# Linear attention and a Sinkhorn-routed mixture of experts: fp16, transposes by DMA, and attention pipelined with the first expert

## The chip, the cores and the metric

The kernel runs on one core of one Trainium2 chip. The metric is device time in microseconds (us), as the median of several executions; lower is better. All executions that are compared here were of the same, undisturbed state ("fast"). The profile is one execution, taken by the hardware profiler.

Names of engines in the profile: PE is the matmul engine and PEld its weight load, DVE the vector engine, ACT the scalar engine, POOL the GpSimd engine, SP the sync engine. "SPq" or "POOLq" is the same engine issuing a DMA.

## The reference

Eight batches, 8 heads, 576 positions, head width 64; then 4608 tokens of width 512 through 8 experts of hidden width 1024, all in fp32.

```python
def phi(x, c, s):                       # c, s: cos and sin of the position
    r = np.maximum(x, 0.0)
    return np.concatenate([r * c, r * s], axis=-1)        # 64 -> 128 features
q_p, k_p = phi(q, cos_w, sin_w), phi(k, cos_w, sin_w)
kv  = np.einsum('bhsf,bhsd->bhfd', k_p, v)
z   = np.sum(k_p, axis=2)
num = np.einsum('bhsf,bhfd->bhsd', q_p, kv)
den = np.einsum('bhsf,bhf->bhs', q_p, z)[..., None] + 1e-06
x   = (num / den) rearranged to (4608 tokens, 512)

P = np.exp(x @ w_gate - max)            # 4608 x 8
for _ in range(8):                      # Sinkhorn
    P /= P.sum(1, keepdims=True) + 1e-09
    P /= P.sum(0, keepdims=True) + 1e-09
    P *= N / E
for e in range(8):
    out += P[:, e:e + 1] * (np.maximum(x @ w1[e], 0.0) @ w2[e])
```

## The kernel before

It runs in three stages, one after the other: attention for all batches, which leaves x transposed in SBUF (`xT`); gates and Sinkhorn; the experts. The parts that matter here:

```python
for b in range(B):
    for hk in range(NPAIR):                            # two heads at a time
        # loads of q, k, v in fp32 on SP's queue, 2304 bytes a row (q: 256)
        nc.scalar.copy(out=q_ld[:, :, 1, :], in_=q_ld[:, :, 0, :])
        nc.vector.tensor_copy(out=v_aug[:, :, 0:D], in_=v_ld[:])      # v and a column of ones
        # k_p = max(k, 0) * (cos | sin), two DVE operations
        for hh in range(2):
            for c in range(CH):                                       # CH = 9
                nc.tensor.matmul(out=kv_ps[:, hh, :], lhsT=k_p[...], rhs=v_aug[...], ...)
        # q transposed on PE, fp32, 9 times; DVE applies max and cos | sin
        nc.tensor.transpose(out=tr_ps[:, i, :], in_=q_ld[:, c], identity=ident_f[:])
        nc.vector.scalar_tensor_tensor(out=q_pT[:, hh, s0:s0+ln], in0=tr_ps[...], ...)
        # numerator and denominator in one matmul; 1/den per token; scaled by ACT into st
        nc.tensor.matmul(out=num_ps[:rows, si, :], lhsT=q_pT[...], rhs=kv_sb[:, hh, :], ...)
        nc.vector.reciprocal(out=rden[...], in_=num_ps[:rows, si, D:D+1])
        nc.scalar.activation(out=st[...], in_=num_ps[...], func=AF.Copy, scale=rden[...])
        nc.tensor.transpose(out=x_ps[...], in_=st[...], identity=ident_bf[...])   # x^T on PE
        # copied to xT
# ... gates, 8 Sinkhorn rounds ...
for e in range(E):                                     # experts outer
    for j in range(NJ):                                # 9 chunks of 512 tokens
        # h_ps (4 buffers) = w1e^T x^T: 32 matmuls of 128x512; ACT: Relu into hT (bf16)
        # y_ps (2 buffers) = hT^T w2e: 32 matmuls of 128x512; DVE: out_acc += P * y_ps
```

The softmax here doesn't subtract the row's maximum and nothing guards it: scores larger than these inputs give would overflow.

## Time and profile before

| | before |
|---|---|
| time, median of 3 executions | 1244.44 us (1241.79 to 1244.47) |
| first expert matmul (`h_ps`) | about 228 us |
| 4608 expert matmuls of 128x512 at 0.2155 us, start to start | 993 us |
| last `y_ps` ends | 1235.4 us of the profiled 1241.5 |

The page of the kernel before. The rows of digits are the span in 40 equal slices, each digit the busy share in tenths; PEclk is the clock granted to PE in tenths. After the chain come groups of instructions: count, then total busy time and mean ns of one, then the idle time before them and who ended it.

```profile
span 1241.5 us, 15196 instructions
PE 1189.6 (96%) x6128; PEld 580.1 (47%) x6128; DVE 431.4 (35%) x1158; ACT 466.3 (38%) x1051; POOL 1.8 (0%) x10
...
PE   5898888899999999999999999999999999999998
...
PEclk9999999999999999999999999999999999999999
DMA  9847440400030003000300030003000100001122
...
PE 89%; DVE 7%; issue 2%; ACT 1%; DMA 0%; SPq 0%; DVEq 0%; ACTq 0%
...
L397 PE MATMUL h_ps<-xT,w1e 128*128 128x512 bf16 x2304 | 515.0, 380 | 0.0
...
L262 PE MATMUL tr_ps<-ident_f,q_ld 128*128 128x128 f32 x288 | 89.1, 440 | 6.3 <-ACT q_ld L213 5.7
...
L247 PE MATMUL kv_ps<-v_aug,k_p 64*128 64x65 bf16 x576 | 43.1, 239 | 31.8 <-DVE k_p L232 24.4
...
L312 PE MATMUL x_ps<-ident_bf,st 128*128 128x128 bf16 (+1 forms) x160 | 33.9, 278 | 4.5 <-ACT st L302 3.0
```

PE is busy 96% of the time, at full clock throughout, and PE is 89% of the chain of work that ended last. But the lines of `tr_ps` and `x_ps` are work that computes nothing: 448 transposes, 123 us of PE busy time. Attention is the first eight slices.

Busy time by stretch of the kernel before: each line is a stretch, its length, then busy us of each engine with the count of instructions, the granted clock, the DMA share and GB/s.

```profile
0.00:100.00 100.00, 75.66 (x552) 51.96 (x552) 70.66 (x332) 53.71 (x187) 1.75 (x10) 1.00 0.77 222
...
400.00:600.00 200.00, 200.00 (x928) 90.69 (x927) 48.92 (x63) 67.18 (x113) 0.00 (x0) 1.00 0.06 22
```

In the attention no engine is full: PE 76, DVE 71 and ACT 54 of 100 us hand work to each other. Among the experts PE is full, and 928 matmuls take 200 us. That stretch is the floor; the 228 us in front of it are what can be won.

### The profile page before, as it was taken

Reading aid. Unit: us, or ns where it says so; the run is one execution under the profiler, and the core shown is the slowest. Engines: PE = TensorE matmul, PEld = TensorE weight load, DVE = VectorE, ACT = ScalarE, POOL = GpSimd, SP = SyncE. Lnnn points to the kernel's source line nnn. Section 1 sums busy time; section 2 is a strip of 40 time slices with the busy share of each in tenths; the row PEclk is TensorE's granted clock in tenths of the full one; section 3 lists DMA queues with packets and bytes.
Section 4 is the critical chain, followed back from the end, with each engine's and each line's share of the span. In section 5 each row is a group of like instructions: output and inputs, shape, how many; then the busy total and the mean of one; then the engine's idle time right before and its main releaser. Section 6 shows DMA issues by size and latency. Waiting matters only on the chain.

```text
span 1241.5 us, 15196 instructions
## 1 busy us (share of the span) xinstructions
PE 1189.6 (96%) x6128; PEld 580.1 (47%) x6128; DVE 431.4 (35%) x1158; ACT 466.3 (38%) x1051; POOL 1.8 (0%) x10
## 2 busy tenths in 40 slices
PE   5898888899999999999999999999999999999998
PEld 3555555444444444444444444444444444444443
DVE  6777777563232223222322232223222322212221
ACT  4554554541333333333333333333333333333332
POOL 0000000000000000000000000000000000000000
PEclk9999999999999999999999999999999999999999
DMA  9847440400030003000300030003000100001122
GB/s 301 218 134 211 127 132 2 137 1 1 1 115 22 1 1 113 23 1 1 112 25 1 1 110 27 1 1 108 29 1 1 68 1 1 1 1 68 68 80 90
DMA packets 64742, 72.30 MB, mean 58 GB/s; under 512 B 39584, under 2 KB 39584, under 8 KB 64672
## 3 DMA queue, kind: packets, MB, share of 16 engines
q1 hardware_dynamic: 64672, 71.33, 18.0%
q8 instruction: 48, 0.79, 0.3%
q14 instruction: 22, 0.18, 0.0%
HBM read 61.88 MB, written 9.44 MB: 57 GB/s over the span
## 4 chain that ended last, share of the span: by engine, by line
PE 89%; DVE 7%; issue 2%; ACT 1%; DMA 0%; SPq 0%; DVEq 0%; ACTq 0%
PE y_ps L413 40%; PE h_ps L397 39%; PE tr_ps L262 4%; PE kv_ps L247 3%; PE num_ps L285 2%; DVE k_p L232 2%; DVE v_aug L227 2%; DVE rden L296 1%; DVE q_pT L270 1%; DVE colp L359 0%; ACT kv_sb L254 0%; DMA v_ld<-in_v_dram 0%; PE x_ps L312 0%; DVE P_tok L352 0%; DVE rs L349 0%
## 5 line engine op out<-in xcount | busy, mean ns | idle before, releaser
L404 ACT ACTIVATE hT<-h_ps 128x512 bf16<-128x512 f32 x576 | 343.9, 597 | 649.7 <-PE h_ps L397 649.0
L397 PE MATMUL h_ps<-xT,w1e 128*128 128x512 bf16 x2304 | 515.0, 380 | 0.0
L413 PE MATMUL y_ps<-w2e,hT 128*128 128x512 bf16 x2304 | 509.2, 379 | 0.0
L430 DVE SCALAR_TENSOR_TENSOR out_acc<-y_ps,P_tok,out_acc 128x512 f32<-128x512 f32 x252 | 189.2, 751 | 620.8 <-PE y_ps L413 620.8
L413 PEld LDWEIGHTS <-hT 128*128 128x128 bf16 x2304 | 225.0, 98 | 271.4
L397 PEld LDWEIGHTS <-w1e 128*128 128x128 bf16 x2304 | 223.9, 98 | 266.1 <-issue 0.3
L262 PE MATMUL tr_ps<-ident_f,q_ld 128*128 128x128 f32 x288 | 89.1, 440 | 6.3 <-ACT q_ld L213 5.7
L302 ACT ACTIVATE st<-num_ps,rden 128x64 bf16<-128x64 f32 (+1 forms) x320 | 70.5, 313 | 42.0 <-DVE rden L296 39.2
L247 PE MATMUL kv_ps<-v_aug,k_p 64*128 64x65 bf16 x576 | 43.1, 239 | 31.8 <-DVE k_p L232 24.4
L270 DVE SCALAR_TENSOR_TENSOR q_pT<-tr_ps,cs2b 128x128 bf16<-128x128 f32 (+1 forms) x320 | 62.9, 260 | 0.2 <-PE tr_ps L262 0.2
L262 PEld LDWEIGHTS tr_ps<-ident_f,q_ld 128*128 128x128 f32 x288 | 48.4, 214 | 11.9 <-issue 5.7
L247 PEld LDWEIGHTS <-k_p 64*128 64x128 bf16 x576 | 32.3, 124 | 42.8 <-DVE k_p L232 28.6
L285 PE MATMUL num_ps<-kv_sb,q_pT 128*128 128x65 bf16 (+1 forms) x320 | 48.2, 251 | 0.2 <-DVE q_pT L270 0.2
L422 DVE TENSOR_SCALAR out_acc<-y_ps,P_tok 128x512 f32<-128x512 f32 x36 | 26.9, 750 | 60.0 <-PE y_ps L413 59.9
L296 DVE RECIPROCAL rden<-num_ps 128x1 f32<-128x1 f32 (+1 forms) x320 | 27.0, 151 | 54.0 <-PE num_ps L285 52.3
L232 DVE SCALAR_TENSOR_TENSOR k_p<-k_ld,cs 128x576 bf16<-128x576 f32 x64 | 45.2, 742 | 0.8 <-ACT cs L147 0.8
L285 PEld LDWEIGHTS <-q_pT 128*128 128x128 bf16 (+1 forms) x320 | 33.1, 134 | 19.0 <-issue 7.0
L312 PE MATMUL x_ps<-ident_bf,st 128*128 128x128 bf16 (+1 forms) x160 | 33.9, 278 | 4.5 <-ACT st L302 3.0
L254 ACT CAST kv_sb<-kv_ps 128x65 bf16<-128x65 f32 x64 | 13.8, 215 | 52.1 <-PE kv_ps L247 49.9
L108 DVE CAST w1e<-wst 128x2048 bf16<-128x2048 f32 x16 | 19.0, 1221 | 36.9 <-PE h_ps L397 36.9
L312 PEld LDWEIGHTS <-st 128*128 128x128 bf16 (+1 forms) x160 | 16.6, 106 | 29.0 <-ACT st L302 16.2
L227 DVE CAST v_aug<-v_ld 128x576 bf16<-128x576 f32 x32 | 23.2, 726 | 4.6 <-DMA v_ld<-in_v_dram 4.6
(62 smaller groups left out, 116.2 us busy)
## 6 DMA issues: line engine op xcount, KB each, us to landing
wst<-in_moe_w_dram SPq DMA_DIRECT2D x32, 1024.0 KB, 5.7
q_ld<-in_q_dram SPq DMA_DIRECT2D x32, 288.0 KB, 3.4
k_ld<-in_k_dram SPq DMA_DIRECT2D x32, 288.0 KB, 3.8
v_ld<-in_v_dram SPq DMA_DIRECT2D x32, 288.0 KB, 3.8
out_dram<-out_acc SPq DMA_DIRECT2D x9, 1024.0 KB, 4.3
wg_ld<-in_moe_w_gate_dram SPq DMA_DIRECT2D x1, 16.0 KB, 1.9
```

Of the source, the lines that this page charges most:

```text
L227: nc.vector.tensor_copy(out=v_aug[:, :, 0:D], in_=v_ld[:])
L232: nc.vector.scalar_tensor_tensor(out=k_p[:, :, a, :], in0=k_ld[:], scalar=0.0, in1=cs[:, :, a, :], op0=ALU.max, op1=ALU.mult,)
L247: nc.tensor.matmul(out=kv_ps[:, hh, :], lhsT=k_p[p0 : p0 + HP, c, :, :].rearrange("p a d -> p (a d)"), rhs=v_aug[p0 : p0 + HP, c, :], star ...
L262: nc.tensor.transpose(out=tr_ps[:, i, :], in_=q_ld[:, c, :, :].rearrange("p a d -> p (a d)"), identity=ident_f[:],)
L270: nc.vector.scalar_tensor_tensor(out=q_pT[:, hh, s0 : s0 + ln], in0=tr_ps[:, i, p0 : p0 + ln], scalar=0.0, in1=cs2b[:, s0 : s0 + ln], op0= ...
L285: nc.tensor.matmul(out=num_ps[:rows, si, :], lhsT=q_pT[:, hh, s0 : s0 + rows], rhs=kv_sb[:, hh, :], start=True, stop=True,)
L302: nc.scalar.activation(out=st[:rows, si, hh * D : (hh + 1) * D], in_=num_ps[:rows, si, 0:D], func=AF.Copy, scale=rden[:rows, si : si + 1],)
L312: nc.tensor.transpose(out=x_ps[:, s0 : s0 + rows], in_=st[:rows, si, :], identity=ident_bf[:rows, :rows],)
L397: nc.tensor.matmul(out=h_ps[:, :ntok], lhsT=w1e[:, kt, ft * P : (ft + 1) * P], rhs=xT[:, kt, tj0 : tj0 + ntok], start=(kt == 0), stop=(kt ...
L404: nc.scalar.activation(out=hT[:, ft, :ntok], in_=h_ps[:, :ntok], func=AF.Relu)
L413: nc.tensor.matmul(out=y_ps[:srows, :], lhsT=hT[:, ft, ts0 : ts0 + srows], rhs=w2e[:, ft, :], start=(ft == 0), stop=(ft == FT - 1),)
L430: nc.vector.scalar_tensor_tensor(out=out_acc[:srows, cidx, :], in0=y_ps[:srows, :], scalar=P_tok[:srows, cidx, e : e + 1], in1=out_acc[:sr ...
```

## The change

Its intent is to take the transposes off PE, and to start expert 0 as soon as a batch of x exists, so that PE has expert matmuls to do while the rest of the attention runs. The diff is large (nearly the whole file); this is its core, shortened, with some lines put in words and cuts marked by "...".

```diff
-BF16 operands, weights loaded in fp32 by SP and cast by DVE
+F16 operands; q, k, v and weights loaded by POOL's queue, cast to fp16 in the DMA
-h_ps: 4 buffers
+h_ps: 2 buffers (the room goes to the attention, which now runs beside it)
 ...
+def prep(b, hk):                       # 4 buffers of k_p, 2 of q_p, 7 of q_pT, 5 of each load
+    nc.vector.tensor_copy(out=v_aug[:, :, 0:D], in_=v16[:])
+    for x16, pool, name in ((k16, kp_pool, "k_p"), (q16, qp_pool, "q_p")):
+        nc.scalar.activation(out=x16[:], in_=x16[:], func=AF.Relu)
+        nc.vector.tensor_tensor(out=x_p[:], in0=x16 (repeated), in1=cs[:], op=ALU.mult)
-        nc.tensor.transpose(out=tr_ps[:, i, :], in_=q_ld[:, c], identity=ident_f[:])
+    nc.sync.dma_start_transpose(out=q_pT[:], in_=q_p[:])           # 128 x 1152 fp16
+    if b + 1 < B:
+        load(b + 1, hk)
+def denominators(b, zsel):
+    # den_ps[head, token]: 24 small matmuls of 192 columns a batch
+    nc.vector.tensor_scalar(out=den[:], in0=den_ps[...], scalar1=1e-6 / XS, op0=ALU.add)
+    nc.vector.reciprocal(out=den[:], in_=den[:])
+    r_dram = dram.tile([H, 3, C3 * HP], FP32, name="r_dram")
+    for j in range(3):
+        nc.sync.dma_start(out=r_dram[:, j, :], in_=den[32 * j : 32 * j + H, :])
+    rb = rb_pool.tile([P, HK, S], FP32, name="rb")                 # 1 buffer, 1.18 MB
+    for hh in range(2):                                            # every row to 64 partitions
+        nc.sync.dma_start(out=rb[hh * HP : (hh + 1) * HP],
+                          in_=r_dram[hh : H : 2]....to_broadcast([HP, HK, S]))
+def attend(b, kv_sb, rb):
+    # num_ps comes out transposed, so that no transpose of x is needed
+    nc.tensor.matmul(out=num_ps[...], lhsT=kv_sb[:, hk, hh, :], rhs=qTs[b, hk][...], ...)
+    nc.vector.tensor_tensor(out=xT[...], in0=num_ps[...], in1=rb[...], op=ALU.mult)
-    nc.tensor.transpose(out=x_ps[...], in_=st[...], identity=ident_bf[...])
+for b in range(B):
+    prep(b + 1, 0..1); attend(b, kv_sb, rb); prep(b + 1, 2..3)
+    ffn2(hT, 0, w0, b - 1, range(2, 4))      # the second half of the last chunk of expert 0
+    kv_sb, zsel = sums(b + 1)                # 72 kv_ps matmuls
+    hT = ffn1(hA, w0, b)                     # 32 h_ps matmuls
+    rb = denominators(b + 1, zsel)
+    gates(...); ffn2(hT, 0, w0, b, range(0, 2))
 ... Sinkhorn, now under the rest of expert 0 ...
+for g in range(NG):                          # expert 0's outputs are gated afterwards
+    nc.gpsimd.tensor_scalar(out=out_acc[:, g, :], ..., scalar1=P_tok[:, g, 0:1], op0=ALU.mult)
+for e in range(1, E): ...                    # experts outer, tokens inner, as before
```

In the changed kernel the profile calls `num_ps`, `den_ps`, the gates' and Sinkhorn's tiles all `small_ps`, because they share a pool; the line number tells them apart (L293 numerator, L260 denominators).

## The prediction

> **What bounds the kernel now.** Read from busy time by stage and the order of time. (1) 0 to about 228 us: attention, before the first expert matmul. In 0:100 PE is busy 76 us, DVE 71, ACT 54; the chain of waits passes through PE transposes, kv_ps, num_ps and DVE's k_p, v_aug, rden. (2) From 228 us the experts: in 400:600, 928 matmuls of 128x512 in 200 us, 0.2155 us each, back to back. 4608 of them are 993 us, a floor that the change does not move. (3) Gates and Sinkhorn (3.69 us a round) run under expert matmuls and cost PE about 13 us. The tail after the last matmul is 6 us, mostly a 1 MB store.
>
> **What changes.**
> - Removed from PE: 288 fp32 transposes of q (89 us busy) and 160 of x (34 us), with their evictions: q_pT (63 us DVE), st (70 us ACT), rden (27 us DVE).
> - Added: 32 DMA transposes of 128x1152; denominators by 192 small matmuls, a reciprocal, a DRAM round trip and a broadcast load of 1.2 MB per batch.
> - Loads cast in the DMA, on POOL's queue.
> - Moved: expert 0's feed-forward runs inside the batch loop, gated later by POOL.
> - h_ps has 2 buffers instead of 4.
>
> **Cost of the new shape.** The built order shows the scheduler running ahead: before the first xT, DVE makes k_p of batches 0 to 3, so 47 loads (13.9 MB) and 4.2 MB of weights must land. At the 300 GB/s of the first 30 us now, that is 60 us (estimate); the late cosine table and the chain transpose, denominator, round trip bring the first expert matmul to about 70 us, instead of 228.
> After it: 993 us of expert matmuls; other PE work in the loop: 360 kv at 0.055 (20 us), 124 num of 288 columns (15), 168 denominators of 192 columns (13), gates (6): 54. Loop stalls: the chain last denominator, add, reciprocal, store, broadcast load (10 to 14 us a batch, estimate) is covered by 13 us of PE work while kv sums remain, 8 in the last batches; xT is paced by 8 DVE operations of about 0.45 us; I allow 25. Sinkhorn stalls 6. h_ps: ACT starts 0.20 us after a group's last issue, takes 0.597, release 0.05: 0.85 of the 0.862 us available, so 6 of stalls. POOL gating 2, tail 4.
> Sum: 70 + 993 + 54 + 25 + 6 + 6 + 2 + 4 = **1160 us**, range 1115 to 1210. Faster by over 2%: 0.88; within: 0.05; slower: 0.07.
>
> **DMA transposes.** The Trainium skill, "DMA: Bandwidth & Descriptors", Latency and other measured facts, gives 261 GB/s for one kernel's DMA transposes; one of 295 KB is then about 1.1 us plus 2 us fixed (estimate); four fit in a batch of 25 us. No trace yet shows it.
>
> **What would show it.** First h_ps matmul near 70 us; Sinkhorn from about 265 us; DMA share high until 60 us, low after; experts 1 to 7 at 13.8 us per 512 tokens; PE idle in the loop mostly before num_ps, released by DVE's xT, behind the rb load.
>
> **What would make it wrong.** A transpose over 6 us makes the queue that also carries rb the bound (32 x 10 = 320 us: slower). Casting loads well below 250 GB/s delay the start by 20 us or more. ACT blocked behind late q loads stalls h_ps. A dearer release costs h_ps up to 0.05 us on 576 groups (29 us).

## The result, and the profile after

| | before | after |
|---|---|---|
| time, median of 4 executions | 1244.45 us (1241.79 to 1246.04) | 1202.43 us (1200.82 to 1204.8) |
| ratio | | 0.9666, 95% interval 0.9647 to 0.9685 |
| predicted | | 1160 us (1115 to 1210) |

A ratio here is the mean time of one kernel's fast runs over that of the other's of the same rounds, so it is not quite the ratio of the medians. The kernel became 3.4% faster; 6.8% had been forecast. The direction and the range held, and half of the gain is missing.

The page of the changed kernel, the lines that answer to those above:

```profile
span 1203.0 us, 13575 instructions
PE 1075.3 (89%) x5680; PEld 481.3 (40%) x5680; DVE 336.8 (28%) x576; ACT 395.3 (33%) x669; POOL 124.1 (10%) x159
...
PE   0247687768999999999999999999999999999998
...
PEclk9998788888999999999999999999999999999999
DMA  9998775571400022000300040004000400003333
...
PE 80%; DMA 13%; issue 3%; DVE 2%; SPq 1%; ACT 1%; POOL 0%; DVEq 0%; ACTq 0%; POOLq 0%
...
L90 PE MATMUL h_ps<-xT,w1e 128*128 128x512 f16 x2304 | 536.5, 387 | 14.8 <-ACT hT L97 14.2
...
L293 PE MATMUL small_ps<-q_pT,kv_sb 128*64 128x288 f16 x128 | 23.6, 414 | 51.5 <-DVE xT L300 51.4
L386 POOL TENSOR_SCALAR out_acc<-out_acc,P_tok 128x512 f32<-128x512 f32 x36 | 55.5, 1555 | 8.9 <-DVE P_tok L373 8.9
L233 PE MATMUL kv_ps<-v_aug,k_p 64*128 64x65 f16 x576 | 14.7, 209 | 34.2 <-DVE k_p L212 29.3
```

PE's busy time fell by 114 us, as intended, but the time by 42. From slice 3 to slice 10 PE is 40 to 80% busy, and from slice 4 its clock is not granted in full. The chain, which had no DMA in it, now has 13%. Note the 51.5 us that PE sat idle in front of L293: the numerators wait for DVE's `xT`, which has to free a `small_ps` buffer.

Busy time by stretch, same columns as before. The cuts are the first expert matmul (76.8 us) and the first Sinkhorn matmul (300.8 us); I call the stretch between them the loop.

```profile
0.00:76.80 76.80, 11.97 (x249) 8.07 (x249) 29.97 (x84) 26.53 (x40) 36.53 (x70) 1.00 1.18 177
76.80:300.80 224.00, 167.41 (x1289) 69.55 (x1288) 94.77 (x190) 63.17 (x117) 22.26 (x41) 0.85 0.63 108
400.00:600.00 200.00, 200.00 (x925) 90.29 (x924) 43.55 (x58) 68.06 (x114) 3.33 (x4) 1.00 0.14 22
```

In the start the DMA engines are crowded: the share is above 1 because packets of one engine overlap in the records. The experts run as before, 0.2155 us a matmul. So the kernel splits cleanly into three: start 76.8, loop 224.1, rest 902 us. The rest lies between 901.9 and 902.3 us in every run (save e8, which puts 3.4 us of extra matmuls there), so from here on start and loop tell the story.

The chain of waits of the changed kernel within one batch, in order of time: start, length, what.

```profile
129.94 0.60 SPq L278
130.54 0.05 issue
130.59 7.41 DMA rb<-r_dram
...
138.10 0.47 DVE xT L300
...
138.61 0.47 PE small_ps L293 x2
...
140.04 7.43 DMA k_1964<-in_k_dram
...
147.58 0.07 ACT k_1964 L210
...
148.16 0.35 ACT kv_sb L250
148.52 0.51 ACT hT L97
149.03 0.04 issue
149.07 3.15 PE h_ps L90 x7
```

Two stories in one batch. First the broadcast load of reciprocals (`rb`) takes 7.4 us, and PE waits for it through `xT`. Then PE waits for ACT, not because ACT is slow, but because ACT's next instruction is the Relu of a `k` that is still being loaded; `hT`, which PE needs, stands behind it in the same queue.

What PE had to do under the first of these waits, from the timeline of the same batch (start, length, engine, line, what, and in brackets the idle time before it):

```profile
131.92 1.31 PE L233 MATMUL kv_ps<-v_aug,k_p 64*128 64x65 f16 x72
...
138.61 0.81 PE L293 MATMUL small_ps<-q_pT,kv_sb 128*64 128x288 f16 x4 [5.38 <-DVE xT L300]
```

The last denominator matmul of this batch ended at 124.0 us and its first `xT` began at 138.1: a chain of 14.1 us (about 1.8 for the addition and the reciprocal, 4.2 for the store to DRAM, 8.2 for `rb`). PE had 9.2 us of work to put over it. In batches 1 to 5 (counted from 0) the chain takes 13.9 to 14.4 us over 9.1 to 9.2 us of work; in the last two it takes 17.4 and 12.1 us over 8. The uncovered rest is 38.8 us in these seven batches.

PE's start-to-start times of matmuls in the loop, added up from the trace: intervals over 0.45 us come to 76.9 us: 28.5 after a `kv_ps` matmul and 15.4 after a `y_ps`, all in front of `num_ps`; 26.6 after `h_ps`, of which 12.9 are in front of `num_ps` too; 6.4 after `den_ps`. By what they stand in front of, they are 56.8 before `num_ps`, 16.7 before `h_ps` and 3.4 before `den_ps`. Expert matmuls with intervals of 0.26 to 0.45 us (73 of them; 31 at about 0.43, twice the usual) cost another 11.9 us over 0.2155 each, 8.6 of it while the recorded clock stood at half. What is left, 135.3 us, is 99.4 of expert matmuls and 35.9 of other PE work. The long intervals also hold 7.5 us of expert matmuls themselves, so the loop comes apart into 106.9 us of expert matmuls, 35.9 of other PE work and about 81 of stalls.

The waits of the changed kernel: who waited for what, us in total, times, longest.

```profile
DVE q_p L212 <- DMA q_pT<-q_p: 56.9, 23, 6.3
PE small_ps L293 <- DVE xT L300: 51.4, 8, 9.9
```

DVE waits 57 us for DMA transposes, because there are only two buffers of `q_p` and a transpose has to read one before DVE may write the next.

### The profile page after: what moved, and what is told of

The parts are those of the page before. It is cut to its first block, busy times and chain, and to the rows that moved or that the text cites. A ratio compares the mean times of both kernels' runs of the same rounds, so it can differ in the third digit from the quotient of the medians.

```text
span 1203.0 us, 13575 instructions
## 1 busy us (share of the span) xinstructions
PE 1075.3 (89%) x5680; PEld 481.3 (40%) x5680; DVE 336.8 (28%) x576; ACT 395.3 (33%) x669; POOL 124.1 (10%) x159
## 4 chain that ended last, share of the span: by engine, by line
PE 80%; DMA 13%; issue 3%; DVE 2%; SPq 1%; ACT 1%; POOL 0%; DVEq 0%; ACTq 0%; POOLq 0%
PE h_ps L90 40%; PE y_ps L105 38%; DMA q_pT<-q_p 4%; DMA rb<-r_dram 4%; DMA w1e<-in_moe_w_dram 1%; PE small_ps L293 1%; DMA q_742<-in_q_dram 1%; DMA k_1964<-in_k_dram 1%; DMA r_dram<-den 1%; SPq L219 0%; DMA q_118<-in_q_dram 0%; ACT hT L97 0%; DMA q_1084<-in_q_dram 0%; DMA v_191<-in_v_dram 0%; DMA q_1001<-in_q_dram 0%
## 5 line engine op out<-in xcount | busy, mean ns | idle before, releaser
L97 ACT ACTIVATE hT<-h_ps 128x512 f16<-128x512 f32 x576 | 342.6, 597 | 643.7 <-PE h_ps L90 643.4
L90 PE MATMUL h_ps<-xT,w1e 128*128 128x512 f16 x2304 | 536.5, 387 | 14.8 <-ACT hT L97 14.2
L105 PE MATMUL y_ps<-w2e,hT 128*128 128x512 f16 x2304 | 510.9, 379 | 0.0
L90 PEld LDWEIGHTS <-w1e 128*128 128x128 f16 x2304 | 225.3, 99 | 298.0 <-issue 47.0
L105 PEld LDWEIGHTS <-hT 128*128 128x128 f16 x2304 | 223.9, 98 | 269.0 <-issue 1.6
L293 PE MATMUL small_ps<-q_pT,kv_sb 128*64 128x288 f16 x128 | 23.6, 414 | 51.5 <-DVE xT L300 51.4
L386 POOL TENSOR_SCALAR out_acc<-out_acc,P_tok 128x512 f32<-128x512 f32 x36 | 55.5, 1555 | 8.9 <-DVE P_tok L373 8.9
L233 PE MATMUL kv_ps<-v_aug,k_p 64*128 64x65 f16 x576 | 14.7, 209 | 34.2 <-DVE k_p L212 29.3
L300 DVE TENSOR_TENSOR xT<-small_ps,rb 128x288 f16<-128x288 f32 x64 | 27.1, 454 | 31.3 <-DMA rb<-r_dram 19.8
L293 PEld LDWEIGHTS <-kv_sb 128*64 128x64 f16 x128 | 7.4, 125 | 69.1 <-DVE xT L300 45.4
L114 DVE COPY out_acc<-y_ps 128x512 f32<-128x512 f32 x36 | 24.8, 690 | 29.7 <-PE y_ps L105 29.7
L260 PE MATMUL small_ps<-q_pT,zsel 128*32 128x192 f16 x192 | 11.1, 276 | 21.3 <-DVE zsel L244 19.2
L260 PEld LDWEIGHTS <-zsel 128*32 128x32 f16 x192 | 5.8, 101 | 32.5 <-DVE zsel L244 19.7
```

What stands on the lines that cost most here:

```text
L90: nc.tensor.matmul(out=h_ps[:], lhsT=w[0][:, kt, ft * P : (ft + 1) * P], rhs=xT[:, kt, j * TCH : (j + 1) * TCH], start=(kt == 0), stop=(kt ...
L97: nc.scalar.activation(out=hT[:, ft, :], in_=h_ps[:], func=AF.Relu)
L105: nc.tensor.matmul(out=y_ps[:], lhsT=hT[:, ft, ts * P : (ts + 1) * P], rhs=w[1][:, ft, :], start=(ft == 0), stop=(ft == FT - 1),)
L114: nc.vector.tensor_copy(out=out_acc[:, g, :], in_=y_ps[:])
L233: nc.tensor.matmul(out=kv_ps[:, hh, hk * (D + 1) : (hk + 1) * (D + 1)], lhsT=k_p[hh * HP : (hh + 1) * HP, c].rearrange("p a d -> p (a d)") ...
L260: nc.tensor.matmul(out=den_ps[32 * j : 32 * j + 32, 0 : C3 * HP], lhsT=zsel[:, h, :], rhs=qTs[b, hk][:, j * C3 : (j + 1) * C3, hh * HP : ( ...
```

## The experiments

Three theories at the outset, about the 38 us by which the loop exceeds the forecast. A: the broadcast load of reciprocals. B: ACT held up by the Relus of k and q. C: the transposes. Two rivals came later: D, too few `q_pT` buffers; E, PE work itself paces the loop. Later expectations name further theories (T, O, Q, R), and say there what they are. In all tables "start" is the first `h_ps` matmul and "loop" from there to the first Sinkhorn matmul, read from each run's trace. Every run was timed against the kernel before on the same chip; three chips were used, and the median of the kernel before was 1244.6 to 1245.1 us on each. The trace of the changed kernel is of the slowest of its four executions (1204.8 us, 2.4 above the median), so a difference of start and loop can be a little larger than that of the medians.

| run | correct | time, us | ratio to before | start | loop |
|---|---|---|---|---|---|
| the changed kernel | yes | 1202.43 | 0.9666 | 76.8 | 224.1 |
| e1_rb_fp16 | yes | 1176.83 | 0.9463 | 70.3 | 206.7 |
| e2_relu_on_dve | yes | 1201.18 | 0.9658 | 68.3 | 226.2 |
| e3_qp_4_buffers | yes | 1205.2 | 0.9699 | 76.5 | 224.3 |
| e4_plain_copy | no | 1185.04 | 0.9523 | 67.5 | 213.1 |
| e5_rb16_qt8 | yes | 1178.45 | 0.9475 | 68.9 | 204.4 |
| e6_denominators_early | yes | 1174.8 | 0.9449 | 75.8 | 194.2 |
| e7_rb16_qt8_early | yes | 1175.08 | 0.9445 | 71.7 | 202.8 |
| e8_extra_y_matmuls | yes | 1210.33 | 0.972 | 77.0 | 221.5 |
| e9_early_plain | no | 1152.41 | 0.9257 | 67.4 | 179.2 |
| e10_early_relu | yes | 1187.17 | 0.9546 | 69.7 | 211.5 |
| e11_early_rb16_ld6 | yes | 1170.77 | 0.9412 | 72.2 | 194.3 |
| e12_early_relu_plain | no | 1161.28 | 0.9331 | 61.9 | 195.4 |
| e13_early_qp4 | yes | 1168.27 | 0.9381 | 78.0 | 186.7 |
| e14_early_rb16_ld6_qp4 | yes | 1151.3 | 0.9265 | 74.5 | 176.5 |

### e1_rb_fp16: half the bytes of the broadcast load

```diff
-nc.vector.reciprocal(out=den[:], in_=den[:])
-r_dram = dram.tile([H, 3, C3 * HP], FP32, ...);  rb = rb_pool.tile([P, HK, S], FP32, ...)
+nc.vector.reciprocal(out=den16[:], in_=den[:])          # den16 is F16
+r_dram = dram.tile([H, 3, C3 * HP], F16, ...);   rb = rb_pool.tile([P, HK, S], F16, ...)
```

> Correct result; the reciprocal, its round trip through DRAM and the broadcast load are fp16, so the load is 0.59 MB a batch instead of 1.18 MB. Theory A (the broadcast load, 7.4 to 9.3 us after its issue, is what PE waits for before num_ps: 51 us of waits on xT): the load lands in 4 to 5.5 us, PE's wait on xT falls to about 30 us, time falls by 18 to 28 us against the changed kernel (1202), to about 1180. Theory B (PE waits because ACT is blocked behind Relus whose loads are late): less than 8 us gained, the wait moves to h_ps. Theory C (DMA transposes are slow): no change, within 4 us.

Measured: 1176.83 us, 25.6 less than the changed kernel, and still correct. In the loop the load lands 4.4 to 5.2 us after its issue instead of 7.4 to 9.3, and PE's wait, in the list of waits of this run, is under half of 51.4:

```profile
PE small_ps L294 <- DVE xT L301: 23.2, 8, 5.5
```

What follows: the load is a large part of the missing gain. The start is 6.5 us shorter too: batch 0 has such a load in front of its first `xT`.

### e2_relu_on_dve: take the waiting Relus out of ACT's queue

```diff
-nc.scalar.activation(out=x16[:], in_=x16[:], func=AF.Relu)
+nc.vector.tensor_scalar(out=x16[:], in0=x16[:], scalar1=0.0, scalar2=None, op0=ALU.max)
```

> Correct result; the Relu of k and q goes from ACT to DVE, so that ACT holds only expert evictions, kv_sb and Exp. Theory B: h_ps intervals over 0.45 us in 76:300 (26.6 us now) almost vanish, time falls by 15 to 25 us, to about 1182. Theory A: under 8 us gained, because the broadcast load still ends last in each batch. Theory C: no change or slower, since DVE then waits for the same late loads.

Measured: 1201.18 us, no gain. The start fell by 8.5 us, but the loop did not, because the wait moved to the engine that now holds the Relus. The waits of this run:

```profile
PE small_ps L295 <- DVE xT L302: 63.1, 10, 10.6
...
DVE q L210 <- DMA q<-in_q_dram: 35.8, 17, 4.0
```

DVE now sits in front of a load, and `xT`, which PE needs, stands behind it. Theory B is true of the mechanism (an in-order engine that waits for a load holds up everything behind) and the move is no remedy: on DVE the waiting instruction holds up `xT` instead.

### e3_qp_4_buffers: more room for the transposes' inputs

```diff
-qp_pool = tc.tile_pool(name="qp_pool", bufs=2)
+qp_pool = tc.tile_pool(name="qp_pool", bufs=4)
```

> Correct result; q_p has 4 buffers instead of 2, so a q_p need not wait for the transpose two before it. Theory C (transposes with 2 buffers pace q_p, hence the q loads and the start): DVE's wait of q_p on q_pT falls from 57 us to under 20, first h_ps moves from 76.8 us to 65 or less, q loads come earlier and time falls by 12 to 25 us. Theory A and B: first h_ps moves by less than 5 us, time within 6 us.

Measured: 1205.2 us; start and loop as before the edit. DVE's wait for transposes fell from 56.9 to 17.8 us, and PE's wait for `xT` stayed at 51.7. Removing DVE's largest wait for a DMA was worth nothing here. I took it as the end of this theory; e13 and e14 show that it was not, since the `rb` wait was hiding it.

### e4_plain_copy: the same bytes without transposing (wrong result)

```diff
-nc.sync.dma_start_transpose(out=q_pT[:], in_=q_p[:]....)
+nc.sync.dma_start(out=q_pT[:], in_=q_p[:]....)
```

> Wrong result on purpose: each DMA transpose is replaced by a plain DMA of the same bytes between the same tiles. Theory C in the form that the crossbar itself is slow: landing falls from about 4 us to 2 or 3, start and loop shorten by 15 us or more. Otherwise (the cost is the DMA round trip and the buffers, or not the transposes at all): within 8 us of 1202.

Measured: 1185.04 us, 17.4 less by the medians: 9.3 us less at the start, 11.0 less in the loop. Theory C holds in this form (the landing times were not compared). The relative error is 0.40, as it should be. Added up over all packets before Sinkhorn, the transposes of the changed kernel take 63.8 us of time of all 16 DMA engines (36,864 packets of 256 bytes); the plain copies take 24.5 (68.0 for their and `rb`'s 2304-byte packets together, less the 43.5 of `rb`). At the start, where the DMA share is over 1, the transposes' packets take 19.8 us, the copies' 7.4 (11.5 less `rb`'s 4.1), and 9.3 us of that difference show in the time.

One rival this run does not separate: the copies go in packets of 2304 bytes, the transposes in packets of 256. The kernel before loads q, without a transpose, in as many packets of 256 bytes; these took 42.7 us of all 16 engines, and their median of 18 ns a packet is the transposes' median too. So about half of the difference between 63.8 and 24.5 us may be packet size and not transposing (an estimate, from loads that come from DRAM and ran beside other traffic).

### e5_rb16_qt8: an eighth q_pT buffer on top of e1

```diff
+(all of e1)
-qT_pool = tc.tile_pool(name="qT_pool", bufs=7)
+qT_pool = tc.tile_pool(name="qT_pool", bufs=8)
```

> Correct; e1 plus 8 buffers of q_pT instead of 7, so that all four transposes of the next batch can go before attention of this one has released a buffer. Theory D (after e1, the rest of the loop's stalls is a chain: num_ps releases q_pT, three transposes of up to 8 to 10 us, q_p, q load, ACT, h_ps): h_ps gaps fall from 26 to under 15 us, time 5 to 15 us below e1 (1177). Rival (late loads themselves, whatever frees the buffers): within 4 us of e1.

Measured: 1178.45 us, as e1 (ratios 0.9475 and 0.9463, with overlapping intervals). Theory D falls.

### e6_denominators_early: the same load, issued earlier

```diff
+rb = denominators(b + 1, zsel)       # before, not after, the 32 h_ps matmuls
 hT = ffn1(hA, w0, b)
-if b + 1 < B:
-    rb = denominators(b + 1, zsel)
```

> Correct; the changed kernel with fp32 rb untouched, only the denominators of the next batch are emitted before this batch's first expert layer instead of after it, which gives the round trip 7 us more PE work to hide under. Theory A (the round trip through DRAM is exposed because too little PE work follows the denominators): waits of PE on xT fall from 51 to under 25 us, time falls by 15 to 30 us, to about 1180, with the rb loads as long as before. Rival (the DMA traffic of rb, 9.4 MB more, delays other loads): no gain, within 6 us, since the traffic is the same.

Measured: 1174.8 us, 27.6 less, with the fp32 load and all its traffic kept. The loop fell by 29.9. Waits of this run:

```profile
DVE q_p L212 <- DMA q_pT<-q_p: 50.8, 16, 6.6
...
PE small_ps L293 <- DVE xT L300: 21.8, 8, 8.5
...
PE h_ps L90 <- ACT hT L97: 16.6, 14, 2.9
```

With e1 this shows theory A from two sides: a shorter load, and a load of the same size issued 32 expert matmuls (6.9 us) earlier, take away about the same.

### e7_rb16_qt8_early: both remedies, and the extra buffers

```diff
+(e1, e5 and e6 together, and rb_pool with 2 buffers)
```

> Correct; e1, 8 buffers of q_pT, denominators early, 2 buffers of rb: the candidate for a better version. Theory A and D together: PE hardly waits on xT (under 10 us), loop from the first h_ps to the first Sinkhorn matmul 170 to 195 us instead of 224, time 1145 to 1168. If the loop is bound by the transposes and loads instead: no better than e1 and e5, about 1175.

Measured: 1175.08 us. This missed: I had expected the remedies to add up at least in part, and the result is e6's. PE no longer waits after `kv_ps` at all (its intervals over 0.45 us are 0 there), but those after `h_ps` grew to 30.4 us and those after `y_ps` are 17.1. So once `rb` is out of the way, something else holds the loop near 195 to 205 us.

### e8_extra_y_matmuls: more PE work in front of the wait

```diff
-for ft in range(FT):
+for rep in range(2 if e == 0 and ts >= 2 and j < B else 1):   # the group is done twice
+  for ft in range(FT):
     nc.tensor.matmul(out=y_ps[:], lhsT=hT[...], rhs=w[1][:, ft, :], ...)
```

> Correct result; in the batch loop the y_ps matmuls of half the tokens of expert 0 are done twice (128 more matmuls of 128x512, 27.6 us of PE time at 0.2155), placed before the wait on xT. Theory A (PE is idle there, the DMA round trip sets the pace): time rises by under 8 us or falls, as the clock stays up and the half-rate intervals shrink. Theory E (PE work itself paces the loop): time rises by 24 to 28 us.

Measured: 1210.33 us. 128 more expert matmuls are 27.6 us of PE work at full rate, and they cost 8 us by the medians. 112 of them, 24.1 us, fall into the loop, which even became 2.6 us shorter in the profiled execution (the fastest of its four). The mean clock rose from 0.971 to 0.989, since PE idles less. Theory E falls: in the loop of the changed kernel PE is not the pace, it has idle time to give away.

### e9_early_plain: what is left once rb is hidden (wrong result)

```diff
+(e6 and e4 together)
```

> Wrong result on purpose: denominators early (fp32 reciprocals) and each DMA transpose replaced by a plain copy of the same bytes. Theory T (with the broadcast load hidden, the transposes are what is left: late at the start, and holding q_p and so DVE in the loop): the start falls by about 9 us and the loop by 10 or more, 1150 to 1160. Theory O (loads of k and q waited for by an in-order engine bind the loop): only the start gains, 1163 to 1168, and the loop stays at about 194.

Measured: 1152.41 us, 22.4 less than e6: 8.4 at the start, 15.0 in the loop. Theory T holds. This is also the forecast, missed by 8 us the other way: without the wait for `rb` and with transposes as cheap as copies, the kernel lands near what I had predicted.

### e10_early_relu: e2 again, with rb hidden

```diff
+(e6 and e2 together)
```

> Denominators early, Relu of k and q on DVE instead of ACT. Theory O in the form that ACT's queue is what holds PE (h_ps waits for an ACT that waits for k or q): gaps before h_ps and y_ps fall from 33 us to under 18, 1158 to 1167. Rival: any in-order engine that waits for the loads passes the wait on; then the waits move to DVE (xT, v_aug, zsel) and the time stays at 1170 to 1180.

Measured: 1187.17 us, 12.4 more than e6; worse than either theory allowed. The loop is 17.3 us longer. A line of its waits says why:

```profile
PE y_ps L105 <- DVE out_acc L114: 26.4, 5, 8.7
```

DVE's copy of `y_ps`, which frees one of two buffers, now stands behind Relus that wait for loads. DVE serves PE in more places (`xT`, `k_p`, `zsel`, `y_ps`) than ACT (`hT`, `kv_sb`, the gates); the waiting instructions are better off on ACT.

### e11_early_rb16_ld6: deeper loads

```diff
+(e6 and e1 together)
-ld = tc.tile_pool(name="ld", bufs=5)
+ld = tc.tile_pool(name="ld", bufs=6)
```

> Denominators early, fp16 reciprocals, 6 load buffers of each of k, v, q instead of 5. If the depth of the loads (a load is issued only when one of 5 buffers is free) binds the loop: loop 185 or less, 1162 or less. If not: 1170 to 1178, as with the denominators early alone.

Measured: 1170.77 us, within the range of "no". The loop is 194.3, as e6's; the gain over e6 is at the start. The depth of the loads alone does not set the loop.

### e12_early_relu_plain: both (wrong result)

```diff
+(e6, e2 and e4 together)
```

> Wrong result on purpose: denominators early, Relu on DVE, plain copies for transposes. If transposes and ACT's place in the order are two separate costs, this adds both gains: 1140 to 1152. If what is left is the arrival of the loads, it is no faster than the better of its two parts by more than 3 us.

Measured: 1161.28 us: worse than e9 (1152.41), by the same mechanism as e10. The start is the shortest of all, 61.9 us. The two parts do not add up, because Relu on DVE is a loss in the loop.

### e13_early_qp4: e3 again, with rb hidden

```diff
+(e6 and e3 together)
```

> Denominators early, 4 buffers of q_p instead of 2. Theory Q (with the broadcast load hidden, a transpose costs the loop by holding a q_p buffer: DVE's next q_p waits, so the next q load is issued late, ACT waits for it, and PE for ACT): DVE's wait for transposes, 51 us, falls under 20, and the loop falls by 8 us or more from 194, time 1160 to 1167. Theory R (transposes cost DMA time, which the loop lacks, whatever the buffers): loop 190 to 198, 1171 to 1178. At the start no gain by either.

Measured: 1168.27 us, 6.5 less than e6, between the two ranges; the loop fell by 7.5. Waits of this run:

```profile
ACT k L210 <- DMA k<-in_k_dram: 60.4, 23, 12.2
...
ACT q L210 <- DMA q<-in_q_dram: 24.7, 17, 4.9
...
DVE q_p L212 <- DMA q_pT<-q_p: 9.4, 4, 4.0
```

DVE's wait went as theory Q said, and ACT's wait for q loads from 51.4 to 24.7 us; but ACT's wait for k loads went up, from 41.9 to 60.4. It leans to Q and does not settle it alone.

### e14_early_rb16_ld6_qp4: everything that helped

```diff
+(e11 and e3 together)
```

> Everything that helped, in one correct kernel: denominators early, fp16 reciprocals, 6 load buffers, 4 q_p buffers. Theory Q: 1155 to 1164. Theory R: 1168 to 1173, as without the q_p buffers.

Measured: 1151.3 us, ratio 0.9265 (0.9242 to 0.9288), correct: 7.3% faster than before, and about 4% faster than the changed kernel (1151.3 over 1202.43). That is below even theory Q's range. It differs from e11 by the two extra `q_p` buffers alone, and these are worth 19.5 us, 17.8 of them in the loop. Waits of e11, then of this run:

```profile
DVE q_p L212 <- DMA q_pT<-q_p: 35.1, 14, 8.9
...
PE h_ps L90 <- ACT hT L97: 20.3, 11, 5.6
```

```profile
DVE q_p L212 <- DMA q_pT<-q_p: 8.5, 3, 6.9
...
PE h_ps L90 <- ACT hT L97: 8.2, 8, 2.2
```

The stretches of this run, cut at its first expert and first Sinkhorn matmul:

```profile
0.00:74.50 74.50, 12.05 (x248) 7.98 (x248) 26.18 (x73) 26.67 (x40) 34.92 (x67) 1.00 1.18 174
74.50:251.00 176.50, 155.67 (x1290) 68.05 (x1288) 95.07 (x201) 61.85 (x117) 23.84 (x44) 0.95 0.67 113
```

Theory Q holds: in the loop a transpose costs by holding a `q_p` buffer, not by the DMA time it takes (that is little changed here: 60.3 us, against 65.0 in e11). Why the same edit was worth 7.5 us of the loop in e13 and 17.8 here, no run separates. With real transposes (and fp16 reciprocals and deeper loads) this loop is slightly shorter than e9's with plain copies. At the start the transposes' cost stays, as expected.

## Why the prediction was right or wrong

The sum was 70 + 993 + 54 + 25 + 6 + 6 + 2 + 4 = 1160. Put against the three stretches of the trace:

| stretch | predicted | measured | difference |
|---|---|---|---|
| start | 70 | 76.8 | +7 |
| loop | 186 (106.9 of expert matmuls, 54 other PE work, 25 stalls) | 224.1 | +38 |
| rest | 904 | 902 | -2 |

The three differences come to 43 us, the 42 us of the miss. That 1202 still lies in the range is owed to the range's width; the loop alone took 38 us more than the sum allowed.

**Right.** The mechanism: the transposes left PE (busy time down by 114 us), the experts began at 77 instead of 228 us, and they still cost 0.2155 us a matmul. POOL's gating (55.5 us on POOL) and Sinkhorn were free for PE, as foreseen. The two `h_ps` buffers cost about 3 us where 6 were allowed. Casting loads were not slow: 2304 bytes of source took 107 ns, against 93 without a cast (medians of a packet). "PE idle in the loop mostly before num_ps, released by DVE's xT, behind the rb load" is what the trace shows: 56.8 of the 76.9 us of long intervals. Two other signs did not come: Sinkhorn began at 300.8 us, not 265, and the DMA share was not low after 60 us but 0.63 over the whole loop.

**Wrong: the term "Loop stalls: the chain last denominator, add, reciprocal, store, broadcast load (10 to 14 us a batch, estimate) is covered by 13 us of PE work ... I allow 25".** It measured about 81 us: 76.9 of long intervals and 11.9 of slower matmuls, less the 7.5 of expert matmuls inside the long intervals. The other PE work came out at 36 us instead of 54, which hid part of the error. The step that failed is the word "covered": about 9 us of work stood over a chain of 14. Four things made the stalls.

- *The chain was as long as the top of its estimate.* It took 13.9 to 14.4 us in batches 1 to 5, then 17.4 and 12.1, where 10 to 14 had been said; the `rb` load is over half of it. The profile before had 2304-byte packets at 93 ns (medians); those of `rb` took about 185 ns in the loop, twice that, though they read the same few rows again and again. With its 512 packets per batch spread over 16 engines that is 5.9 us (512 x 185 / 16 ns), and it landed 7.4 to 9.3 us after its issue; it was no faster in the last batch, when there were no other loads. e1 and e6 show what it cost: 26 to 28 us.
- *The cover was overestimated.* It was 9.1 to 9.2 us where 13 had been said, and 8 in the last two batches, as said. So PE stood idle for 4 to 9 us in each of seven batches, 38.8 us in all, where the estimate left 0 to 1 us, and 2 to 6 in the last batches. Of the missing 4 us, 2.7 are the `kv_ps` matmuls: I counted 0.055 us for each of the 72 of a batch, and they took 1.31 us in all, 18 ns each. Two 64-row halves alternate here, and the starts follow each other after 3 to 4 and 25 to 30 ns in turn; the kernel before does one half after the other, mostly at 54 to 57 ns. Cheaper work lowered "other PE work" from 54 to 36 us and raised the stall by the same token: work that serves as cover is worth nothing when it gets cheaper.
- *A wait for a transpose travels.* I had asked only whether four transposes fit into a batch, and they do. But with 2 buffers of `q_p`, DVE waits for the transpose; the next q load is issued only after DVE has read the last; ACT waits for that load; PE waits for ACT. The risk "ACT blocked behind late q loads stalls h_ps" was named, and given no us in the sum. Against e11, e14 shows 17.8 us of it in the loop. In the changed kernel itself it is hidden: e3 alone gained nothing, which fits `rb` coming last at the waits.
- *An idle PE is slow when it comes back.* I costed all expert matmuls at 0.2155 us. In the loop 31 took about 0.43. The Trainium skill, "TensorE: Matmul & The Clock Gate", Part 1, says that the default state of the array's clock is half rate and that about 3.4 us of activity release it; the trace agrees, with twice the interval after idle stretches, recorded stretches at half clock of 3.4, 6.8 or 10.2 us, and a granted clock of 0.85 in the loop, where PE is busy 167 of 224 us. e8 raised the clock by giving PE more to do. As a term of the sum this is small: 8.6 us of expert matmuls. (The clock record alone proves little: two executions of the kernel before have a mean of 0.91 and 0.92 in it, at the usual 1246.17 and 1241.28 us. Here the matmuls' intervals show the same.)

**The start (+7).** The DMA share there is 1.18, so the DMA engines are crowded. I had counted the loads and left the transposes out of the traffic. They are not the whole of it: e2 keeps the transposes and starts 8.5 us earlier too, with 12.0 MB moved by then instead of 13.6, so what is let in first counts as well. The estimate of 1.1 us each was worked out from 261 GB/s in the Trainium skill, "DMA: Bandwidth & Descriptors", Latency and other measured facts. In this trace one of 295 KB took 2.0 us of all 16 engines (63.8 us over 32), an estimate of 148 GB/s. Another page, "Advanced Engine Details and Errata", X-Bar Transpose (TRN2), says that transposes are as fast as regular DMAs on TRN2. Here they took 63.8 us against 24.5 for plain copies of the same bytes, and e4 starts 9 us earlier. The measurement decides for these copies; against plain loads in packets of the transposes' own size (42.7 us, see e4) the gap is about half as large.

**What stays open.** e14's loop still has some 32 us of intervals over 0.45 us. No run tells how much of it is the supply of k (ACT still waits for it) and how much the last batches, where one interval in front of `num_ps` stays at 5.8 us. And why a packet of `rb` takes twice the time was measured, not explained: fp16 packets of half the size took 77 to 78 ns on average (e14, e1) against 163 to 170 (e6, the changed kernel), so the time goes with the bytes, which a fixed cost per packet would not do. Reading the same rows is not enough to explain it: the first batch's `rb` packets, beside the loads of the start, had a median of 106 ns.

## What to carry to other kernels

When a serial stage is turned into a pipeline, work out the slowest chain of one turn with its DMA round trips, and what covers it; the saved busy time is only the upper bound. Move the issue of a round trip ahead of the longest block of independent work before making it smaller: here a reordering of two statements was worth as much as halving the load. And test buffers again after each larger wait is removed: two more `q_p` buffers were worth nothing with the `rb` wait in front, 6.5 us with the load issued earlier, and 19.5 us with fp16 reciprocals and a sixth load buffer as well.

## What the Trainium skill lacked or had wrong

- "Advanced Engine Details and Errata", X-Bar Transpose (TRN2), has transposes as fast as regular DMAs. Here 32 transposes of 128x1152 fp16 took 63.8 us of time of 16 DMA engines, plain copies of the same bytes 24.5; replacing them gained 17 us in the changed kernel and 22 with the denominators early. Part of this goes with the packets: 256 bytes against 2304; plain loads in as many 256-byte packets took 42.7 us in the kernel before.
- "DMA: Bandwidth & Descriptors", Latency and other measured facts, gives 261 GB/s for transposes with a non-contiguous middle dimension. Here, beside other traffic, 148 GB/s (an estimate from 9.4 MB and 63.8 us of packet time); transposes that ran with little beside them took 1.53 us, 193 GB/s (an estimate from 295 KB).
- No page that I found has a figure for one DMA that reads the same DRAM rows for many partitions. Here, in the loop, its 2304-byte packets took about 185 ns against 93 for ordinary loads of the kernel before, and 1.18 MB landed 7.4 to 9.3 us after issue (halved to fp16: 4.4 to 5.2 us).
- "TensorE: Matmul & The Clock Gate", Part 1, says that the time from start to start never drops below about 25 ns, however small the matmul. Here 72 matmuls of 65 columns, alternating between two 64-row halves of the array, took 1.31 us, 18 ns each, with starts 3 to 4 and 25 to 30 ns apart in turn. Part 3 of that page has the missing case: about 4 ns between starts in different row groups. So the floor of Part 1 is not one for matmuls that alternate between halves.
